# Windowed attention, gated convolution and gated values on one core: scores in four 64x64 tiles, batch 0 turned by transposes, a tap and the split of v on GpSimd

## The chip, the cores and the metric

The kernel runs on one core of one Trainium2 chip. The metric is device time in microseconds (us). A core has TensorE (PE: matrix products into the accumulators, PSUM, which has 8 banks), VectorE (DVE), ScalarE (ACT), GpSimd (POOL, which does not read PSUM) and SyncE (SP, which here issues all DMAs). PEld is PE's loading of its stationary operand.

## The reference

Three layers, for 4 batches of 576 positions, in float32:

```python
# 1: attention, 8 heads of 64, window 128, linear bias by distance
scores = scale * np.matmul(q, k.transpose(0, 1, 3, 2))
mask = (rel >= 0) & (rel < window)
scores = np.where(mask, scores + bias[None], -1000000000.0)
attn = np.exp(scores - np.max(scores, axis=-1, keepdims=True))
attn = attn / (np.sum(attn, axis=-1, keepdims=True) + 1e-09)
x = np.matmul(attn, v)                       # heads side by side: 512 columns
# 2: h = relu(x @ w_in), 1024 wide; 3 taps along the positions; gate; back to 512
h = np.maximum(x @ w_in, 0.0)
x = h * sigmoid(conv(h, 3 taps)) @ w_out
# 3: value x @ w_val, gated by 5 causal taps over x; out
out = sigmoid(causal_conv(x, 5 taps)) * (x @ w_val) @ w_out2
```

## The kernel before

Features lie on the 128 partitions, positions along the columns. The work is cut into 8 units: 4 batches, each in a first half (positions 0 to 255, `u` = 0) and a second (the rest, `u` = 1). For a unit the loop at L849 records `hidden` (product `win`, ReLU, three taps, gate), `mixed` (product `wout`, five taps), `valued` (product `wval`, times the gate) and `output` (product `wo`, and the DMA of the result), and the attention of the unit after it. Float32 operands of these dense products are split into a high and a low part (fp32r), and L691 to L693 are the three products high x high, high x low, low x high; the weights are split (`widen`, L376) while batch 0 runs. A weight tile comes by DMA into one of three `raw` buffers, ACT writes a part of it into a PSUM bank of `ring_pw`, DVE shifts the other part (L390) and joins the two (L401), and ACT and POOL split the result.

`attention` takes a pair of heads (`p`) and a half. Positions go in blocks of 64, four in the first half and five in the second; a block sees at most 192 keys, and the first two of a sequence 64 and 128. For a block, both heads are computed at once: the stationary matrix (L538) is 128x128 with the queries of one head in one quarter, those of the other in the opposite one, and zeros elsewhere. Two blocks share one of three score banks (`pss`). Then DVE adds the bias and takes the maximum (L542), ACT takes the exponential and its sum (L550), POOL and DVE make the reciprocal (L555, L560). In batches 1 to 3 the rows are scaled and split into two float16 parts (L598, L600), and DMA transposes turn them (L609). In batch 0 (`turn`) they stay in float32 and PE turns them: a product with a diagonal matrix `dg` scales and turns 128 columns at once (L568, L569, L576), and ACT copies the result to `pt`. The value product (L640) uses 128x64 tiles, one head in each half of the array's columns. Its v is float32 in batch 0; after that it is scaled and split into two float16 parts, in most pairs by ACT (L515) and DVE (L355), in eight by ACT and POOL (L509, L512).

The dense products take PSUM banks `pm` in turn: four, but two for the first 16 products, as the other two (`ring_pw`) then serve the weights.

The order is not the order of the code. Each step is recorded with its engine (or several to choose from), an estimated duration, its reads and writes, and a priority. `forward` simulates the engines and takes the readiest step of the best priority; `backward` sets priorities from the end of a simulated run; `order` repeats this 7 times and keeps the best run. The engines then run that fixed order. Where the simulated PE would be idle before 80 us, `warm` puts fillers there: products of an idle tile (L868).

Of the kernel before, what the change touches and what calls it, by code (L numbers as in the profile page):

```python
# [40 lines left out]
class Program:  # L41
# [28 lines left out]
    def forward(self):  # L70
# [24 lines left out]
        while n < len(self.ops):  # L95
# [19 lines left out]
            if o.bank is not None and o.bank in held:  # L115
                x, until = held[o.bank]
                if x != e and until > t:
                    heapq.heappush(wait[e], (until, o.seq, o))
                    continue
            if e == "SP" and dma - t > BACKLOG:  # L120
                heapq.heappush(wait[e], (dma - BACKLOG, o.seq, o))
                continue
            o.eng, o.dur, o.fn = next(a for a in o.alts if a[0] == e)
            out.append(o)
            if e == "PE":
                if tiled and not o.drain:
                    t += 85.0
# [68 lines left out]
    def order(self):  # L196
# [21 lines left out]
BACKLOG = 2500.0  # L218
SLOW = {"DVE": 0.72, "POOL": 0.15}
# [27 lines left out]
def attention_moe_moe_kernel(  # L247
# [51 lines left out]
    ring_raw = Ring("raw", RAWS, [128, 2 * WC], U32)  # L299
    ring_g = Ring("g", 11, [128, 2, GMAX], F32R)  # L300
# [75 lines left out]
    def widen(src, cols, hi, lo, hk, lk, prio):  # L376
# [8 lines left out]
        tk = ps_m.name + str(2 + ring_pw.at)  # L385
# [90 lines left out]
    def attention(b, u, p, prio, step):  # L476
# [27 lines left out]
        if not turn:  # L504
# [21 lines left out]
        groups = [[0, 1], [2, 3]] if nb == 4 else [[0, 1], [2, 3], [4]]  # L526
        for gi, g in enumerate(groups):
            gp, sk = ps_s.next()
            a, e = g[0], g[-1] + 1
            pr = prio + step * (e - 1)  # L530
            blk = []
            for i in g:
                j = j0 + i
                nkey = 64 * min(j + 1, 3)
                blk.append((i, gp[:, 192 * (i - a):192 * (i - a) + nkey], nkey, 64 * (max(0, j - 2) - k0)))

            def scores(blk=blk):
                return [nc.tensor.matmul(out=o, lhsT=q_t[:, i, :], rhs=k_t[:, kc:kc + nkey], start=True, stop=True,  # L538
                                         skip_group_check=True) for i, o, nkey, kc in blk]
            pg.add("PE", sum(mm4_t(b_[2]) for b_ in blk), scores, pr, (qk,), ((sk, 0), (sk, 1)))  # L540
            for i, s, nkey, _ in blk:
                pg.add("DVE", 128 + 1.05 * nkey, lambda i=i, s=s, nkey=nkey: nc.vector.tensor_tensor_reduce(  # L542
                    out=s, in0=s, in1=bm[:, p, 192 - nkey:192], op0=ALU.add, op1=ALU.min,
                    scale=-0.125, scalar=3.0e38, accum_out=stt[:, 0, i:i + 1]), pr, ("bm",), ((sk, i - a), (stk, 0, i)), bank=sk)
            for i, s, nkey, _ in blk:
                to, tok = s, ()
                if turn:
# [4 lines left out]
                    accum_out=stt[:, 1, i:i + 1]), pr, ((stk, 0, i), "pz" + pk[1:]), ((sk, i - a), (stk, 1, i)) + tok, bank=sk)  # L552
# [388 lines left out]
```

## Time and profile before

| | |
|---|---|
| median of 3 runs | 439.55 us (438.98 to 440.91) |
| the profiled execution | 438.07 us, its span 436.3 us |
| busy: PE, DVE, ACT, POOL | 421.0, 323.4, 302.6, 194.7 us |
| granted clock of TensorE | 1.0 in all 40 slices |
| chain that ended last | PE 77%, DVE 10%, POOL 4%, ACT 3%, DMA 3% |

A busy time counts a moment once, however many instructions overlap in it. Matmuls are pipelined: a duration of one is from its start to the end of its drain, and what one costs in a stream is the distance between starts. The page's share of the chain is time on the path that ended last; the stages show where each engine is near full.

### The profile page before, as it was taken

How to read it: one execution, taken by the hardware profiler on the slowest of the kernel's cores; microseconds unless marked ns; L12 is line 12 of the kernel's file. 1: busy time of each engine (PE TensorE's matmuls, PEld its weight loads, DVE VectorE, ACT ScalarE, POOL GpSimd, SP SyncE). 2: the span in 40 equal slices, each digit the busy share in tenths (PEclk: the TensorE clock that was granted, in tenths of full speed). 3: DMA queues.
4: the chain of work that ended last, by engine and by line, in shares of the span. 5: the costliest groups of instructions: out<-in, count | busy, mean ns of one | idle time of the engine just before them, and what ended most of it. 6: DMA issues, size and time to landing. Idle time of an engine off the chain costs nothing.

```text
span 436.3 us, 9827 instructions
## 1 busy us (share of the span) xinstructions
PE 421.0 (96%) x3433; PEld 401.5 (92%) x3433; DVE 323.4 (74%) x1000; ACT 302.6 (69%) x894; POOL 194.7 (45%) x341
## 2 busy tenths in 40 slices
PE   7879899899999999999999999999999999999996
PEld 7669788799999999999999999999999999999996
DVE  4799998987857488947888288938888498817480
ACT  5779787755858586857968587648856687848442
POOL 2568899732634063213713274234604073536311
PEclk9999999999999999999999999999999999999999
DMA  8878566769016437471446337482544446540001
GB/s 278 271 248 287 189 205 224 223 191 233 14 62 109 123 96 169 88 192 36 97 114 134 114 75 175 90 189 86 77 94 107 132 112 137 86 109 0 2 0 63
DMA packets 74738, 57.05 MB, mean 131 GB/s; under 512 B 56000, under 2 KB 65472, under 8 KB 74688
## 3 DMA queue, kind: packets, MB, share of 16 engines
q1 hardware_dynamic: 74688, 56.42, 49.7%
q8 instruction: 27, 0.44, 0.4%
q14 instruction: 23, 0.19, 0.1%
HBM read 38.32 MB, written 4.72 MB: 99 GB/s over the span
## 4 chain that ended last, share of the span: by engine, by line
PE 77%; DVE 10%; POOL 4%; ACT 3%; DMA 3%; issue 2%; SPq 0%; DVEq 0%; ACTq 0%
PE pm L691 22%; PE pm L692 20%; PE pm L693 20%; PE pss L538 8%; PE psx L640 5%; DVE t L355 2%; DVE pss L542 1%; DVE raw L390 1%; DVE dg L568 1%; DVE gts L401 1%; DMA raw<-in_vN 1%; POOL g L370 1%; DMA pt<-p 1%; DVE vmx L435 1%; PE pss L576 1%
## 5 line engine op out<-in xcount | busy, mean ns | idle before, releaser
L691 PE MATMUL pm<-x,win 128*128 128x256 f32 (+1 forms) x256 | 80.0, 313 | 0.4 <-DVE t L355 0.3
L691 PE MATMUL pm<-g,wout 128*128 128x254 f32 (+1 forms) x256 | 80.0, 313 | 0.1
L692 PE MATMUL pm<-g,wout 128*128 128x254 f32 (+1 forms) x256 | 76.2, 297 | 0.0
L692 PE MATMUL pm<-x,win 128*128 128x256 f32 (+1 forms) x256 | 76.1, 297 | 0.0
L693 PE MATMUL pm<-x,win 128*128 128x256 f32 (+1 forms) x256 | 75.8, 296 | 0.0
L693 PE MATMUL pm<-g,wout 128*128 128x254 f32 (+1 forms) x256 | 75.7, 296 | 0.0
L355 DVE SCALAR_TENSOR_TENSOR t<-pm,cc,t 128x325 f32<-128x325 f32 (+3 forms) x112 | 56.7, 515 | 16.3 <-ACT t L348 12.9
L370 POOL TENSOR_TENSOR g<-t,g 128x254 fp32r<-128x254 f32 (+1 forms) x64 | 52.2, 818 | 33.0 <-ACT g L339 30.1
L538 PE MATMUL pss<-qk 128*128 128x192 f32 (+2 forms) x288 | 57.8, 326 | 3.2 <-ACT pt L348 2.1
L355 DVE SCALAR_TENSOR_TENSOR gts<-pm,cc,gts 128x322 f32<-128x322 f32 (+4 forms) x120 | 58.7, 512 | 0.6
L542 DVE CUSTOM_DVE_ANT_0 pss<-pss,bm 128x192 f32<-128x192 f32 (+2 forms) x144 | 48.4, 342 | 10.3 <-PE pss L538 7.8
L550 ACT ACTIVATE pss<-pss,st 128x192 f32<-128x192 f32 (+2 forms) x108 | 41.0, 380 | 14.2 <-DVE st L542 12.5
L691 PEld LDWEIGHTS pm<-x,win 128*128 128x128 f32 x256 | 48.2, 188 | 2.7 <-DVE t L355 1.2
L538 PEld LDWEIGHTS pss<-qk 128*128 128x128 f32 x288 | 45.5, 195 | 5.3 <-ACT pt L348 3.2
L691 PEld LDWEIGHTS pm<-g,wout 128*128 128x128 f32 x256 | 48.2, 188 | 2.2 <-DVE gts L355 1.1
L693 PEld LDWEIGHTS pm<-g,wout 128*128 128x128 f32 x256 | 48.6, 190 | 0.0
L692 PEld LDWEIGHTS pm<-g,wout 128*128 128x128 f32 x256 | 48.6, 190 | 0.0
L692 PEld LDWEIGHTS pm<-x,win 128*128 128x128 f32 x256 | 48.2, 188 | 0.0
L693 PEld LDWEIGHTS pm<-x,win 128*128 128x128 f32 x256 | 48.2, 188 | 0.0
L600 DVE SCALAR_TENSOR_TENSOR p<-pss,st,p 128x192 f16<-128x192 f32 (+1 forms) x103 | 36.4, 388 | 15.1 <-DMA pt<-p 8.9
L555 POOL TENSOR_SCALAR st<-st 128x2 f32<-128x2 f32 (+1 forms) x80 | 16.0, 200 | 69.0 <-ACT pss L550 58.7
L370 POOL TENSOR_TENSOR g<-gts,g 128x254 fp32r<-128x254 f32 (+1 forms) x32 | 26.0, 817 | 37.1 <-ACT g L339 36.3
(100 smaller groups left out, 1092.7 us busy)
## 6 DMA issues: line engine op xcount, KB each, us to landing
qk<-in_qk SPq DMA_DIRECT2D x16, 544.0 KB, 4.0
qk<-in_qk SPq DMA_DIRECT2D x16, 384.0 KB, 3.5
raw<-in_w_out SPq DMA_DIRECT2D x12, 512.0 KB, 4.3
raw<-in_w_in SPq DMA_DIRECT2D x8, 512.0 KB, 5.1
vr<-in_vN SPq DMA_DIRECT2D x14, 256.0 KB, 3.0
out<-t SPq DMA_DIRECT2D x16, 161.0 KB, 1.8
raw<-in_vN SPq DMA_DIRECT2D x6, 384.0 KB, 3.8
raw<-in_w_val SPq DMA_DIRECT2D x4, 512.0 KB, 4.4
```

The lines of the kernel that those rows point to most:

```text
L355: pg.add("DVE", dve_t(n, 0 if isinstance(scalar, float) else 1), lambda: nc.vector.scalar_tensor_tensor(out=out, in0=in0, scalar=scalar, i ...
L370: "POOL": (pool_t(n, True), lambda: nc.gpsimd.tensor_tensor(out=lo, in0=src, in1=hi.bitcast(F32), op=ALU.subtract))}
L390: pg.add("DVE", dve_t(cols, fast=True), lambda: nc.vector.tensor_scalar(low, low, 29, None, op0=ALU.logical_shift_right), prio, (rk,), (rk ...
L538: return [nc.tensor.matmul(out=o, lhsT=q_t[:, i, :], rhs=k_t[:, kc:kc + nkey], start=True, stop=True, skip_group_check=True) for i, o, nke ...
L542: pg.add("DVE", 128 + 1.05 * nkey, lambda i=i, s=s, nkey=nkey: nc.vector.tensor_tensor_reduce(out=s, in0=s, in1=bm[:, p, 192 - nkey:192], ...
L550: pg.add("ACT", act_t(nkey, True, 2), lambda i=i, s=s, to=to: nc.scalar.activation(out=to, in_=s, func=AF.Exp, scale=-1.0, bias=stt[:, 0, ...
L555: "POOL": (165, lambda a=a, e=e: nc.gpsimd.tensor_scalar(stt[:, 2, a:e], stt[:, 1, a:e], 1e-9, norm, op0=ALU.add, op1=ALU.mult))}
L600: pg.add("DVE", dve_t(nkey, 1), lambda i=i, s=s, hi=hi, lo=lo: nc.vector.scalar_tensor_tensor(out=lo, in0=s, scalar=stt[:, 2, i:i + 1], in ...
L640: r.append(nc.tensor.matmul(out=oap, lhsT=lhs, rhs=rhs, start=(i == first[h]), stop=(i == last[h]), skip_group_check=True))
L691: return [nc.tensor.matmul(out=o, lhsT=wh, rhs=hi, start=first, stop=False), nc.tensor.matmul(out=o, lhsT=wh, rhs=lo, start=False, stop=Fa ...
L692: nc.tensor.matmul(out=o, lhsT=wh, rhs=lo, start=False, stop=False),
L693: nc.tensor.matmul(out=o, lhsT=wl, rhs=hi, start=False, stop=last)]
```

## The change

- `attention`: in batches 1 to 3 the first four blocks of a half are one group (`quad`). Each block is two 64x64 products (one head each, no zeros), both written to the block's bank; blocks 0 and 2 use one score bank, 1 and 3 another, so a group holds two of the three. In odd blocks the heads' places in the partitions are exchanged, with a second bias table `bx` (loaded into `raw2` once the weights are in) and other offsets in the value product. The fifth block of the second half is done as before.
- batch 0: the exp rows are scaled in place on DVE, POOL or ACT, and turned by PE transposes with the unit matrix; the `dg` ring goes, and `p` has two buffers.
- `mixed`: the first tap added (k = 3) goes by ACT and POOL in every batch, not in batch 0 alone. v's scaling, cast and subtraction are all POOL's in batches 1 to 3.
- the dense products have three banks for the first 16, and the weights one.
- the planner: DVE steps on the port shared with POOL do not start under a POOL step and the two exclude each other; other estimates for the scores and the turns; 41 simulated runs, from the tenth on with random changes to the priorities.

```diff
@@ forward
+            if e == "DVE" and o.port and using["POOL"] > t + SPIN:
+                heapq.heappush(wait[e], (using["POOL"] - SPIN, o.seq, o))
+                continue
...
-                if tiled and not o.drain:
+                if tiled and tiled != o.drain:
                     t += 85.0
...
-                x = "DVE" if e == "POOL" else "POOL"
-                both = max(0.0, using[x] - t)
...
+                t = max(t, using["DVE" if e == "POOL" else "POOL"])
@@ order
-        for i in range(1 + 6):
+        rng = random.Random(1)
+        for i in range(1 + 40):
             if i:
                 self.backward(span)
+            if i > 8:
+                for o in self.ops:
+                    o.prio += rng.gauss(0.0, 200.0)
@@ buffers
+    ring_vm = Ring("raw", 0, None, None)
+    ring_vm.t = ring_raw.t[0:2]
+    bx = ring_raw.t[2][:, 0:NP * 96].bitcast(BF16).rearrange("q (p n) -> q p n", n=192)
...
-    ring_p = Ring("p", 1, [128, 2, 10, 128], F16)
-    ring_dg = Ring("dg", 3, [128, 128], F32)
+    ring_p = Ring("p", 2, [128, 2, 10, 128], F16)
...
-    ps_m.spare = (16, 16)
+    ps_m.spare = (16,)
...
-    ring_pw.t = ps_m.t[2:4]
+    ring_pw.t = ps_m.t[3:4]
@@ attention: v
-            if nth_a in (18, 20, 21, 23, 24, 29, 30, 31):
-                pg.add("ACT", act_t(n, False, 1), lambda: nc.scalar.activation(out=vin, in_=vin, func=AF.Copy, scale=s_up),
+            if nth_a > 7:
+                pg.add("POOL", pool_t(n,False,1), lambda: nc.gpsimd.tensor_scalar(vin, vin, s_up, 0.0, op0=ALU.mult, op1=ALU.add),
                        prio, ((sck, 1),), vkeys)
-                cast(vin, v1, n, prio, vkeys, ((vk, 1), vk))
+                cast(vin, v1, n, prio, vkeys, ((vk, 1), vk), ('POOL',))
@@ attention: scores
+            held = [ps_s.next() for _ in range(2 if four else 1)]
...
+                o, ok = held[i % 2] if four else held[0]
+                c = 192 * (i // 2 if four else i - a)
...
+                    for h in range(2):
+                        x = h ^ (i % 2)
+                        r.append(nc.tensor.matmul(
+                            out=o[64 * x:64 * x + 64], lhsT=q_t[64 * h:64 * h + 64, i, 64 * h:64 * h + 64],
+                            rhs=k_t[64 * h:64 * h + 64, kc:kc + nkey], start=True, stop=True, skip_group_check=True))
@@ attention: batch 0
-                        lambda dg=dg, ri=ri: nc.vector.tensor_scalar(dg, eye, ri, None, op0=ALU.mult),
-                        lambda dg=dg, ri=ri: nc.gpsimd.tensor_scalar(dg, eye, ri, 0.0, op0=ALU.mult, op1=ALU.add)),
+                        lambda row=row, ri=ri: nc.vector.tensor_scalar(row, row, ri, None, op0=ALU.mult),
+                        lambda row=row, ri=ri: nc.gpsimd.tensor_scalar(row, row, ri, 0.0, op0=ALU.mult, op1=ALU.add),
+                        lambda row=row, ri=ri: nc.scalar.activation(out=row, in_=row, func=AF.Copy, scale=ri)),
...
-                        return [nc.tensor.matmul(out=gp[:, 128 * (x - 2 * a):128 * (x - 2 * a) + 128], lhsT=pe_[:, 128 * x:128 * x + 128],
-                                                 rhs=dg, start=True, stop=True, skip_group_check=True) for x in sl]
+                        return [nc.tensor.transpose(gp[:, 128 * (x - 2 * a):128 * (x - 2 * a) + 128], pe_[:, 128 * x:128 * x + 128], eye)
+                                for x in sl]
@@ mixed
-                    k in ((3,) if b == 0 else ()), yk)
+                    k == 3, yk)
```

On PE, at scores of a first half among dense products; before this is batch 2 (`pss` is a score bank, `qk` a pair's queries and keys, `x` and `g` inputs of dense products; x2 is a count):

```order
L693 MATMUL pm_119<-x_88,win_62 128x328
L538 MATMUL pss_124<-qk_103 128x64
L538 MATMUL pss_124<-qk_103 128x128
L691 MATMUL pm_120<-x_92,win_61 128x328
L692 MATMUL pm_120<-x_92,win_61 128x328
L693 MATMUL pm_120<-x_92,win_62 128x328
L691 MATMUL pm_120<-x_88,win_61 128x328
L692 MATMUL pm_120<-x_88,win_61 128x328
L693 MATMUL pm_120<-x_88,win_62 128x328
L538 MATMUL pss_125<-qk_103 128x192 x2
L538 MATMUL pss_123<-qk_104 128x64
```

On PE after the change, at scores of batch 1:

```order
L726 MATMUL pm_119<-g_82,wout_63 128x254
L727 MATMUL pm_119<-g_82,wout_64 128x254
L562 MATMUL pss_123<-qk_103 64x64 x2
L562 MATMUL pss_121<-qk_103 64x128 x2
L562 MATMUL pss_123<-qk_103 64x192 x2
L562 MATMUL pss_121<-qk_103 64x192 x2
L725 MATMUL pm_119<-g_83,wout_63 128x254
L726 MATMUL pm_119<-g_83,wout_63 128x254
L727 MATMUL pm_119<-g_83,wout_64 128x254
```

A pair's four blocks stood apart, two in one bank and two in the next, with dense products between; now the eight products of four blocks stand together, in two banks.

On DVE in batch 0, at the first weights and the softmax of the first pairs; before (`st` holds maxima, sums and reciprocals, `raw` weights, `cc` and `gts` joined weights):

```order
L568 TENSOR_SCALAR dg_115<-eye,st_111 128x128
L542 ISA pss_125,st_112<-pss_125,bm 128x128
L542 ISA st_112 128x1
L401 SCALAR_TENSOR_TENSOR cc<-pm_121,raw_74 128x44
L390 TENSOR_SCALAR raw_75<-raw_75 128x512
L560 RECIPROCAL st_111<-st_111 128x2
L401 SCALAR_TENSOR_TENSOR gts<-pm_122,raw_75 128x512
```

On DVE after the change, at the same place:

```order
L597 TENSOR_SCALAR p_113<-p_113,st_111 128x64
L396 TENSOR_SCALAR raw_75<-raw_75 128x512
L396 TENSOR_SCALAR raw_74<-raw_74 128x44
L588 RECIPROCAL st_111<-st_111 128x2
L597 TENSOR_SCALAR p_113<-p_113,st_111 128x192
L407 SCALAR_TENSOR_TENSOR cc<-pm_120,raw_74 128x44
```

The diagonal matrix is gone from DVE's order; it scales a row of `p` here instead, and the weights' shifts come in pairs ahead of their joins. Of the 36 rows, 8 stand on DVE, 11 on POOL and 17 on ACT; PE's order has 122 fillers where it had 85.

On POOL, in the second half of batch 0, as v of batch 1 is prepared; before (`vr` is v as loaded, `v` its two parts, `vsc` its scale):

```order
L370 TENSOR_TENSOR g_86<-t_98,g_86 128x326
L678 CAST x_90<-x_91 128x2x8
L370 TENSOR_TENSOR g_87<-t_99,g_87 128x326
L366 TENSOR_TENSOR t_101<-t_101,t_93 128x326
L370 TENSOR_TENSOR g_77<-t_100,g_77 128x326
L555 TENSOR_SCALAR st_111<-st_111 128x2
```

On POOL after the change, at the same place:

```order
L515 TENSOR_SCALAR vr_105<-vr_105,vsc 128x256
L347 TENSOR_SCALAR v_106<-vr_105 128x256
L376 TENSOR_TENSOR g_87<-t_99,g_87 128x326
L518 TENSOR_TENSOR v_106<-vr_105,v_106 128x256
L712 CAST x_90<-x_91 128x2x8
L372 TENSOR_TENSOR t_101<-t_101,t_93 128x326
L376 TENSOR_TENSOR g_77<-t_100,g_77 128x326
```

The three steps of v stand between the splits of the gated products and ahead of `x`'s copy; the normalisation that ends the first piece comes later in the order.

## Rows read from the trace of the kernel before

**Rows 1.** The page: busy us, share and instructions by engine; the chain by engine.
```profile
PE 421.0 (96%) x3433; PEld 401.5 (92%) x3433; DVE 323.4 (74%) x1000; ACT 302.6 (69%) x894; POOL 194.7 (45%) x341
...
PE 77%; DVE 10%; POOL 4%; ACT 3%; DMA 3%; issue 2%; SPq 0%; DVEq 0%; ACTq 0%
```
**Rows 2.** Stages (us from:to): length, busy and instructions by engine, granted clock, DMA.
```profile
0.00:24.00 24.00, 18.67 (x130) 15.78 (x131) 15.17 (x58) 15.25 (x50) 11.07 (x29) 1.00 0.82 278
24.00:62.60 38.60, 34.77 (x290) 30.63 (x288) 36.40 (x106) 32.47 (x94) 31.24 (x45) 1.00 0.73 235
62.60:83.20 20.60, 18.65 (x161) 17.41 (x159) 17.46 (x49) 16.36 (x40) 18.20 (x27) 1.00 0.66 218
83.20:145.00 61.80, 61.55 (x455) 58.92 (x455) 47.50 (x136) 40.35 (x119) 25.26 (x41) 1.00 0.52 126
145.00:376.00 231.00, 230.90 (x1975) 223.92 (x1975) 177.95 (x589) 167.38 (x518) 86.57 (x167) 1.00 0.49 113
376.00:436.30 60.30, 56.42 (x430) 54.83 (x428) 28.88 (x68) 30.81 (x77) 22.40 (x35) 1.00 0.23 47
```
**Rows 3.** The chain in order of time, batch 0 to 1: start, us, what.
```profile
127.43 0.65 PE pss L538 x4
...
128.98 0.44 PE pss L538 x4
```
**Rows 4.** Timeline of PE around a value product in batch 0: start, us, what.
```profile
83.98 0.28 PE L693 MATMUL pm<-g,wval 128*128 128x254 f32 x1
84.19 1.32 PE L640 MATMUL psx<-pt,v 128*64 128x128 f32 x20
...
85.67 0.28 PE L692 MATMUL pm<-g,wval 128*128 128x254 f32 x1
```
**Rows 5.** The turns, as a group (busy, mean ns), and eight in the timeline.
```profile
L576 PE MATMUL pss<-dg,p 128*128 128x128 f32 x128 | 19.1, 283 | 1.8 <-POOL dg L569 1.1 <-DVE dg L568 0.8
...
35.24 1.05 PE L576 MATMUL pss<-dg,p 128*128 128x128 f32 x8
36.13 0.58 PE L868 MATMUL psx<-idle 128*128 128x192 bf16 x5
```
**Rows 6.** Twelve fillers in the timeline, and what follows them.
```profile
15.65 1.15 PE L868 MATMUL psx<-idle 128*128 128x192 bf16 x12 [0.93 <-ACT x L655]
16.64 1.81 PE L576 MATMUL pss<-dg,p 128*128 128x128 f32 x12
```
**Rows 7.** Lines: ns min/median/max, first and last; then groups: busy, mean ns.
```profile
L568 DVE TENSOR_SCALAR dg<-eye,st x18: 273/600/1336, 7.5 to 75.7; 128x128 f32<-128x128 f32 x18
L390 DVE TENSOR_SCALAR raw<-raw x25: 190/424/1528, 6.3 to 80.5; 128x512 uint32<-128x512 uint32 x24, 128x44 uint32<-128x44 uint32 x1
...
L568 DVE TENSOR_SCALAR dg<-eye,st 128x128 f32<-128x128 f32 x18 | 10.8, 621 | 0.7 <-PE pss L576 0.7
L390 DVE TENSOR_SCALAR raw<-raw 128x512 uint32<-128x512 uint32 x24 | 15.9, 664 | 0.0
L339 ACT ACTIVATE p<-t 128x192 f16<-128x192 f32 x3 | 1.0, 364 | 0.0
```
**Rows 8.** Timeline of POOL and DVE at 41.7 us.
```profile
41.66 1.27 POOL L370 TENSOR_TENSOR wout<-gts,wout 128x512 fp32r<-128x512 f32 x1
41.70 1.53 DVE L390 TENSOR_SCALAR raw<-raw 128x512 uint32<-128x512 uint32 x1
```
**Rows 9.** Groups of the widening on ACT and DVE.
```profile
L401 DVE SCALAR_TENSOR_TENSOR gts<-pm,raw 128x512 uint32<-128x512 uint32 x24 | 16.2, 680 | 1.8 <-POOL wval L370 1.2 <-ACT pm L392 0.3
...
L392 ACT ACTIVATE pm<-raw 128x512 f32<-128x512 f32 (+1 forms) x25 | 15.5, 625 | 0.1
```
**Rows 10.** Groups on POOL: a tap's addition, the cast and subtraction of v.
```profile
L366 POOL TENSOR_TENSOR gts<-gts,t 128x253 f32<-128x253 f32 (+1 forms) x8 | 6.8, 846 | 7.3 <-ACT t L365 7.3
...
L341 POOL TENSOR_SCALAR v<-vr 128x512 f16<-128x512 f32 x5 | 3.1, 620 | 6.0 <-ACT t L348 3.0 <-ACT vr L509 2.5 <-PE psx L640 0.4
L512 POOL TENSOR_TENSOR v<-vr,v 128x512 f16<-128x512 f32 x6 | 7.0, 1166 | 0.3
```

More of the change, by code (lines that the diff above doesn't have):

```diff
@@ L1 @@
+import random
 from contextlib import ExitStack
@@ L218 @@
 BACKLOG = 2500.0
+SPIN = 150.0
+XP = 75.0
 SLOW = {"DVE": 0.72, "POOL": 0.15}
@@ L384, in widen @@
         pw, _ = ring_pw.next()
[L385 removed]
+        tk = ps_m.name + str(3 + ring_pw.at)
         r = raw.rearrange("p (n w) -> p n w", w=2)
@@ L428, in vmax @@
         for pp in groups:
-            raw, rk = ring_raw.next()
+            raw, rk = ring_vm.next()
             np_ = len(pp)
@@ L525, in attention @@
         norm = 1.0 if turn else 1.0 / PSC
-        groups = [[0, 1], [2, 3]] if nb == 4 else [[0, 1], [2, 3], [4]]
+        quad = not turn
+        if quad:
+            groups = [[0, 1, 2, 3]] if nb == 4 else [[0, 1, 2, 3], [4]]
+        else:
+            groups = [[0, 1], [2, 3]] if nb == 4 else [[0, 1], [2, 3], [4]]
         for gi, g in enumerate(groups):
-            gp, sk = ps_s.next()
             a, e = g[0], g[-1] + 1
             pr = prio + step * (e - 1)
-            blk = []
+            four = len(g) == 4
+            held = [ps_s.next() for _ in range(2 if four else 1)]
+            gp, sk = held[0]
+            blk, on = [], {}
+            every = tuple((y, x) for _, y in held for x in range(2))
             for i in g:
@@ L534, in attention @@
                 nkey = 64 * min(j + 1, 3)
[L535 to L540, printed above, removed]
+                o, ok = held[i % 2] if four else held[0]
@@ new lines, in attention, with scores @@
+                c = 192 * (i // 2 if four else i - a)
+                on[i] = (ok, i // 2 if four else i - a)
+                blk.append((i, o[:, c:c + nkey], nkey, 64 * (max(0, j - 2) - k0)))
+            def scores(blk=blk, four=four):
+                r = []
+                for i, o, nkey, kc in blk:
+                    if not four:
+                        r.append(nc.tensor.matmul(out=o, lhsT=q_t[:, i, :], rhs=k_t[:, kc:kc + nkey], start=True, stop=True,
+                                                  skip_group_check=True))
+                        continue
+                    for h in range(2):
[3 more added lines that the diff above has]
+                            rhs=k_t[64 * h:64 * h + 64, kc:kc + nkey], start=True, stop=True, skip_group_check=True))
+                return r
@@ L541, in attention @@
+            dur = sum(max(mm4_t(x[2]) for x in blk[y:y + 2]) for y in (0, 2)) + 60 if four else sum(mm4_t(b_[2]) for b_ in blk)
+            pg.add("PE", dur, scores, pr, (qk,), every).drain = "quad" if four else False
             for i, s, nkey, _ in blk:
-                pg.add("DVE", 128 + 1.05 * nkey, lambda i=i, s=s, nkey=nkey: nc.vector.tensor_tensor_reduce(
-                    out=s, in0=s, in1=bm[:, p, 192 - nkey:192], op0=ALU.add, op1=ALU.min,
-                    scale=-0.125, scalar=3.0e38, accum_out=stt[:, 0, i:i + 1]), pr, ("bm",), ((sk, i - a), (stk, 0, i)), bank=sk)
+                tab, tk = (bx, (("bx", 0), ("bx", 1))) if four and i % 2 else (bm, ("bm",))
+                pg.add("DVE", 75 + 1.05 * nkey, lambda i=i, s=s, nkey=nkey, tab=tab: nc.vector.tensor_tensor_reduce(
+                    out=s, in0=s, in1=tab[:, p, 192 - nkey:192], op0=ALU.add, op1=ALU.min,
+                    scale=-0.125, scalar=3.0e38, accum_out=stt[:, 0, i:i + 1]), pr, tk, (on[i], (stk, 0, i)), bank=on[i][0])
@@ L581, in attention @@
                 to = pt32[:, s0:slots[-1] + 1:st_, :]
-                scaled(to, src, 1.0, 128 * sn, pr, ((sk, 0), (sk, 1)), ((ptk, 0, gi),), ("ACT",), True, sk)
+                scaled(to, src, 1.0, 128 * sn, pr, every, ((ptk, 0, gi),), ("ACT",), True, sk)
                 continue
@@ L847, in attention_moe_moe_kernel @@
         load(n)
+    for x in range(2):
+        sync(lambda x=x: nc.sync.dma_start(out=bx[64 * x:64 * x + 64], in_=bias[64 - 64 * x:128 - 64 * x]),
+             90000.0, (), (("bx", x), "raw2", "raw2l"), 273.0)
     t, todo = T0, UNITS
```

30 lines of the change are left out of this document (15 added, 15 removed).

## The prediction, made before the changed kernel had run

> **What bounds the kernel now.** I read the busy times of the engines first, then those by stage, then the chain of waits, and only then single pieces. TensorE (PE) is busy 96% of the span, and the chain that ended last is 77% PE [rows 1]. The stages say where this holds. I cut the span where batch 0, first half of the positions, begins its val product (83.2 us) and at 376 us, where the last attention work ends. Between the two, PE is busy 292.45 of 292.8 us while VectorE (DVE) has 225 and GpSimd (POOL) 112: what PE is spared there comes off the end, and what another engine is spared is worth nothing [rows 2]. Before 83.2 us it is otherwise: in 24 to 62.6 us DVE is busy 36.4 of 38.6 us (94%), against 90, 84 and 81% for PE, ACT and POOL; and part of PE's work in these early stages is fillers on an idle tile [rows 2, 6]. So the change is two sums: PE work after 83.2 us, and the length of the stage before it.
>
> **Scores in 64x64 tiles.** Batches 1 to 3 have 12 head pairs for each half. Today two score blocks of 192 keys cost PE 0.65 us and a pair of 64 and 128 keys 0.44 [rows 3]; four blocks are 0.65 + 0.65 = 1.30 us in the second half of the positions and 0.44 + 0.65 = 1.09 in the first. Each block multiplies a 128x128 matrix that is half zeros. The change does eight 64x64 products instead, and they are meant to run four at a time: two rounds, 2 x 0.325 = 0.65 us in the second half, and in the first half a round of at most 128 keys (0.22) and one of 192 (0.325), 0.54.
>
> The trace has no 64x64 tiles, but it has 128x64 ones, in the value product of batch 0. From 83.98 to 85.67 us stand one dense step before, twenty instructions, and one dense step after; with 0.12 us for each of the two steps, the visit takes 1.45 us [rows 4]. Each head has 640 columns, which at 0.325/192 = 1.69 ns a column is 1.08 us. Two heads one after the other would be 2.17. So the two halves of the array do work at once, and a visit to another tile shape costs about 1.45 - 1.08 = 0.37 us for leaving the dense stream and coming back. With that a four-block group costs 0.65 + 0.37 = 1.02 (saves 0.28) or 0.54 + 0.37 = 0.91 (saves 0.18), and 12 x 0.46 = 5.5 us come off. The fifth block of the second half stays as it is.
>
> Bounds. If the visits cost nothing, 12 x (0.65 + 0.55) = 14.4 us come off. If only two products run at a time, groups cost 1.30 + 0.37 and 1.09 + 0.37, and 12 x 0.74 = 8.9 us are added. If none overlap, 2.60 + 0.37 and 2.18 + 0.37: 12 x 3.1 = 38 us added. I take 5.5, since the nearest row shows halves of the array overlapping.
>
> Here a rule of the Trainium skill speaks against the change. TensorEngine Tiling (Array Packing), section Gotcha 1: PSUM Pressure, says that tiles on different rows of the array write different PSUM banks and cannot reach one bank at the same time. The diff puts both heads of a block, which are different row tiles, into one bank (in different partitions); by the rule as worded they would take turns, and the sum would be the +8.9 us above instead of -5.5. The rows here show column tiles alone, so they neither bear it out nor refute it.
>
> **Turning by transposes, batch 0.** There are 64 of these 128x128 turns, each two instructions [rows 5]. Eight instructions take 36.13 - 35.24 = 0.89 us, or 0.22 a turn [rows 5]. The trace has no transpose on PE; I take one instruction for the two, 0.11, the middle between no gain (two instructions as now) and 14.2 us (free): 64 x 0.11 = 7.1 us less PE work. All of it lies before 83.2 us. The order also has 122 fillers where there were 85; a filler costs (16.64 - 15.65)/12 = 0.083 us [rows 6], so 3.1 us come back. PE's stream before 83.2 us is 4.0 us shorter, if nothing else holds it.
>
> The diagonal matrices go: 18 on DVE, 10.8 us, and 18 on POOL. DVE's cost a mean of 621 ns and at best 273 [rows 7]; the excess is waiting for POOL, as in the shift of 1.53 us that ends 0.30 us after the POOL operation it started beside [rows 8]. In their place the 36 exp rows are scaled: 8 on DVE, 11 on POOL, 17 on ACT by the order. At 0.36 us on ACT and 0.42 on DVE (the nearest rows, a cast of 192 columns and the median shift [rows 7]) DVE gets back 3.4 us and ACT 6.2. The 24 shifts of the weights have a median of 424 ns and a mean of 664 [rows 7]; the new planner no longer starts DVE work on that port under a POOL operation, and of 24 x 0.24 = 5.8 us I take half. DVE's sum before 83.2 us, 69.0 us [rows 2], falls by 10.8 - 3.4 + 2.9 = 10.3. ACT's, 64.1, rises by 6.2, less some 2 for four scalings by channel weights that the order moves off it.
>
> What is late next: ACT. In 24 to 62.6 us it would have about 35 busy us (32.5, 3.6 for ten of the rows, less 1), and filled as densely as DVE is now (94%) needs 37.3 of the 38.6. So the stage shrinks by at least 1.3 us and at most by what DVE loses, 10.3; the middle is 5.8, and PE's own 4.0 lies beside it. I take 6. Two edits are inside this number. The dense products of the first half of batch 0 (16 of them) get three banks instead of two, so a product can begin while two others still are read. The widening of the weights gets one bank instead of two: a bank is held for an ACT pass of 0.63 us and a DVE pass of 0.68 [rows 9], so 24 in a row need at least 24 x 1.31 = 31 us of the 83, and they wait more tightly on DVE. Two buffers for the exp rows let one pair's exponentials start before the other's are turned.
>
> **One tap, and v's split, to POOL.** In batches 1 to 3, 24 taps leave DVE; each becomes an ACT pass and a POOL addition of 0.85 us [rows 10]. All 24 splits of v go to POOL: a scaling and a cast at 0.62 us and a subtraction of 1.17 for 512 columns, 2.4 us [rows 10], and some 1.5 for 256. Together 24 x 0.85 + 12 x 2.4 + 12 x 1.5 = 67 us, less some 12 for the eight splits that POOL has now. POOL after 83.2 us rises from 134 to 189 of 353 us, 54% [rows 2]. I price it at nothing: PE's dense stream covers it. Behind a split on POOL's queue wait the normalisation of softmax, and with it the copies and DMA transposes, and then PE. The cover is gone when the order's lead is less than the 2.4 us; 24 such waits of half that would cost 29 us, and the low end is nothing.
>
> **The sum.** The profiled execution took 438.07 us (span 436.3): 438.07 - 5.5 - 6.0 = 426.6. The median of the runs, 439.55, is 1.5 above the profiled one, so I predict 428.0 us, and 423 to 433 for this case by itself.
>
> **Rivals.**
> *Batch 0 keeps its length.* ACT takes DVE's place, or the single bank makes the widening late, and only the scores pay: 439.5 - 5.5 = 434. For it speaks that ACT and POOL are above 80% in the middle stage; against it, that nothing there is added to POOL and PE loses work.
> *Batch 0 gives all that DVE loses.* 10.3 us, and the visits to the score tiles share their cost with those of the value product beside them, a third of 24 x 0.37 (3 us): 439.5 - 10.3 - 5.5 - 3 = 420.7. For it speak the 94% of DVE and the stalls on POOL.
> *Tiles take turns.* In the four-block groups of batches 1 to 3 only two products run at once; +8.9 there and -6 in batch 0 give 442.5, slower. It decides from where the 24 groups cost more than 28.7 us (now) + 6 = 34.7, or 1.45 us for one. Speaking against it are the overlapping halves [rows 4].
> *PE waits in the stream.* A group takes two of the three score banks until all four blocks are read, where a pair took one, and normalisation queues behind v's split. If each of the 24 groups makes PE wait 0.4 us, 9.6 us go: 428 + 9.6 = 437.6. Against it: PE's stream idles 0.35 us of 292.8 now.
>
> **Chances.** Forecast 0.55; batch 0 unchanged 0.19; all of DVE 0.14; tiles in turn 0.08; PE waits 0.04. A difference within 0.5% (2.2 us) can't be told from none. The forecast, the second and the third case are faster but for about 0.04 at the edge: 0.84. That edge and the last case are the same: 0.08. Tiles in turn are slower: 0.08. The range takes in the first three cases and the last: 419 to 438.
>
> **What would show it.** In the changed profile: score groups of 0.9 to 1.1 us in the chain, with four instructions starting almost together; from the first val product on, PE still without idle; that product at about 77 us instead of 83.2; transposes of one instruction at about 0.11 us; DVE below 90% and ACT near 90% in the middle stage; POOL near 245 us busy. The forecast is wrong if groups take over 1.45 us, if idle time of PE after 83 us passes 3 us, or if the first val product is no earlier.

## The result, and the profile after

The changed kernel takes 433.09 us (median of four runs, 430.77 to 434.29) against 439.55: a ratio of 0.984, 95% interval 0.981 to 0.987. It is faster, by 6.5 us where 11.5 were forecast; 433.1 lies in the range of 419 to 438, and just outside the forecast's own 423 to 433. The profiled execution took 433.56 us (span 431.8).

The page's busy times and TensorE clock (40 slices), and the chain by engine; they answer to [rows 1]:

```profile
PE 413.1 (96%) x3598; PEld 382.5 (89%) x3598; DVE 305.6 (71%) x941; ACT 296.1 (69%) x900; POOL 239.8 (56%) x392
...
PEclk9999989999999999999999999999999999999999
...
PE 67%; DVE 15%; DMA 6%; ACT 5%; issue 3%; POOL 2%; ACTq 0%; DVEq 0%; POOLq 0%
```

PE is as full as before, but its share of the chain is down from 77% to 67%, and one slice of the clock is below full. The stages cut as in [rows 2] (length, then PE, PEld, DVE, ACT, POOL, the granted clock, DMA):

```profile
24.00:62.60 38.60, 33.78 (x282) 30.46 (x282) 32.82 (x96) 33.53 (x98) 28.33 (x42) 0.96 0.71 232
62.60:83.20 20.60, 19.59 (x188) 17.61 (x187) 17.69 (x52) 17.24 (x46) 16.74 (x22) 1.00 0.66 215
83.20:145.00 61.80, 58.08 (x445) 53.74 (x444) 46.51 (x127) 38.47 (x115) 32.25 (x52) 1.00 0.53 137
145.00:376.00 231.00, 229.63 (x2189) 213.90 (x2188) 169.75 (x560) 165.21 (x529) 127.34 (x216) 1.00 0.51 116
```

Before, PE idled 0.35 us between 83.2 and 376 us; now it idles 61.80 - 58.08 + 231.00 - 229.63 = 5.1. In the middle stage DVE is down from 94% to 85%, ACT is at 87%, and the clock is 0.96.

The pieces that the prediction had priced, from PE's timeline and (the last row) from the chain, where a piece counts only its time on the path:

```profile
77.25 0.28 PE L725 MATMUL pm<-g,wval 128*128 128x254 f32 x1
...
237.37 0.31 PE L727 MATMUL pm<-g,wo 128*128 128x322 f32 x1
237.61 0.88 PE L562 MATMUL pss<-qk 64*64 64x192 f32 x16
238.42 0.42 PE L725 MATMUL pm<-g,wo 128*128 128x322 f32 x1
238.67 0.32 PE L726 MATMUL pm<-g,wo 128*128 128x322 f32 x1
```
```profile
59.52 0.66 PE pss L606 x6
```

The first val product stands at 77.25 us, where about 77 was forecast. From 237.37 to 238.67 us lie two dense steps of 0.15 us and a score group: 1.30 - 0.30 = 1.00 us for four blocks (forecast 1.02; two pairs took 1.30). The first instructions of its four tiles start 6 to 7 ns apart. The same reading of the first half's groups gives 0.90 (forecast 0.91). A transpose takes 0.66 / 6 = 0.11 us (taken as 0.11).

So both terms of the sum arrived, and some was given back. I number PE's dense steps in order of time, the first as 0; a batch has 576. Step 576, where batch 0 is over by count, begins at 147.5 us (148.2 before): of the 6.0 us won at the val product, 5.3 are lost again by then. From there to the start of the last dense step it takes 280.6 us instead of 284.3. Two places in batch 0 stand out. The first, in windows:

```profile
48.00:51.00 3.00, 3.00 (x34) 2.77 (x29) 3.00 (x10) 2.98 (x11) 3.00 (x4) 1.00 0.84 240
51.00:54.40 3.40, 0.03 (x2) 0.03 (x1) 3.33 (x10) 3.37 (x11) 3.07 (x6) 1.00 0.89 282
54.40:58.10 3.70, 3.70 (x25) 3.43 (x25) 2.46 (x6) 2.79 (x8) 3.54 (x4) 0.54 0.80 230
58.10:61.00 2.90, 2.90 (x27) 2.90 (x27) 1.72 (x4) 0.79 (x2) 0.67 (x2) 1.00 0.55 167
```
```profile
54.37 3.70 PE L905 MATMUL psx<-idle 128*128 128x192 bf16 x23 [3.37 <-DVE x L691]
```

PE stands still for 3.4 us: the next things on its queue are 23 fillers, and these wait for DVE to read the value product out of the bank that they write. Then they run at a granted clock of 0.54, that is nearly at the lower level, 1.2 GHz, and take 3.70 us (0.16 each against 0.083 in [rows 6]), with the `wout` products behind them. The second place is 93 to 131 us; before, then after:

```profile
93.00:131.00 38.00, 37.84 (x274) 36.65 (x273) 28.94 (x72) 24.61 (x66) 14.56 (x20) 1.00 0.41 105
93.00:131.00 38.00, 34.73 (x269) 31.17 (x268) 31.59 (x85) 25.23 (x75) 18.64 (x30) 1.00 0.60 152
```

The stretch from step 288 to step 480 takes 38.3 us where it took 32.4. Its waits, in brackets:

```profile
95.99 0.42 PE L725 MATMUL pm<-x,win 128*128 128x328 f32 x1 [0.62 <-ACT t L354]
100.64 0.38 PE L456 MATMUL psx<-eye,vmx 128*4 128x128 f32 x2 [0.97 <-DVE vmx L450]
...
107.33 0.38 PE L470 MATMUL psx<-vdg,one 4*128 4x8 f32 x2 [0.45 <-DVE vdg L466]
122.95 0.30 PE L674 MATMUL psx<-pt,v 128*64 128x256 f16 x2 [1.05 <-DMA pt<-p]
```

Two of them, 1.42 of these 3.09 us, are the scale of v, which needs the maxima loaded through two raw buffers, one fewer than before.

### The profile page after: what moved, and what is told of

It is laid out like the page before. It is cut to its first block, busy times and chain, and to the rows that moved or that the text cites. A ratio compares the mean times of both kernels' runs of the same rounds, so it can differ in the third digit from the quotient of the medians.

```text
span 431.8 us, 10151 instructions
## 1 busy us (share of the span) xinstructions
PE 413.1 (96%) x3598; PEld 382.5 (89%) x3598; DVE 305.6 (71%) x941; ACT 296.1 (69%) x900; POOL 239.8 (56%) x392
## 4 chain that ended last, share of the span: by engine, by line
PE 67%; DVE 15%; DMA 6%; ACT 5%; issue 3%; POOL 2%; ACTq 0%; DVEq 0%; POOLq 0%
PE pm L725 19%; PE pm L726 17%; PE pm L727 17%; PE psx L674 4%; DMA raw<-in_vN 4%; DVE t L361 4%; PE pss L562 4%; PE pss L557 3%; DVE gts L361 2%; PE psx L905 2%; DVE pss L570 2%; DMA pt<-p 1%; DVE gts L407 1%; ACT p L578 1%; ACT pm L761 1%
## 5 line engine op out<-in xcount | busy, mean ns | idle before, releaser
L361 DVE SCALAR_TENSOR_TENSOR gts<-pm,cc,gts 128x322 f32<-128x322 f32 (+3 forms) x96 | 47.0, 508 | 2.0 <-POOL gts L372 0.8
L372 POOL TENSOR_TENSOR gts<-gts,t 128x253 f32<-128x253 f32 (+1 forms) x32 | 25.8, 806 | 28.4 <-ACT t L371 18.0
L630 DVE SCALAR_TENSOR_TENSOR p<-pss,st,p 128x192 f16<-128x192 f32 (+2 forms) x103 | 35.9, 386 | 7.8 <-ACT p L628 7.5
L570 DVE CUSTOM_DVE_ANT_0 pss<-pss,bm 128x192 f32<-128x192 f32 (+2 forms) x96 | 32.4, 342 | 11.4 <-PE pss L557 8.2
L725 PE MATMUL pm<-g,wval 128*128 128x254 f32 (+1 forms) x128 | 39.6, 310 | 0.2 <-ACT g L345 0.2
L725 PE MATMUL pm<-g,wo 128*128 128x254 f32 (+1 forms) x128 | 38.9, 304 | 0.3 <-DVE gts L820 0.3
L726 PE MATMUL pm<-g,wo 128*128 128x254 f32 (+1 forms) x128 | 38.1, 298 | 0.2 <-POOL g L376 0.2
```

Source lines behind the costliest of these rows:

```text
L361: pg.add("DVE", dve_t(n, 0 if isinstance(scalar, float) else 1), lambda: nc.vector.scalar_tensor_tensor(out=out, in0=in0, scalar=scalar, i ...
L372: pg.add("POOL", pool_t(n, True), lambda: nc.gpsimd.tensor_tensor(out=out, in0=out, in1=t, op=ALU.add), prio, (tk,), (key,))
L570: pg.add("DVE", 75 + 1.05 * nkey, lambda i=i, s=s, nkey=nkey, tab=tab: nc.vector.tensor_tensor_reduce(out=s, in0=s, in1=tab[:, p, 192 - nk ...
L630: pg.add("DVE", dve_t(nkey, 1), lambda i=i, s=s, hi=hi, lo=lo: nc.vector.scalar_tensor_tensor(out=lo, in0=s, scalar=stt[:, 2, i:i + 1], in ...
L725: return [nc.tensor.matmul(out=o, lhsT=wh, rhs=hi, start=first, stop=False), nc.tensor.matmul(out=o, lhsT=wh, rhs=lo, start=False, stop=Fa ...
L726: nc.tensor.matmul(out=o, lhsT=wh, rhs=lo, start=False, stop=False),
```

## The experiments

The theory at the start: quads are worth 5.5 us, and what was lost sits in the late maxima of v. Rivals: quads bring little; POOL's split of v holds PE up; the order drawn by the planner decides. All times are medians beside runs of the kernel before (439.2 to 439.6 us).

**E1, full scores.**

```diff
-        quad = not turn
+        quad = False
```

> The changed kernel, with the scores of batches 1 to 3 in 128x128 products of two blocks as before; everything else as changed. Theory (quads are worth what the sum says, 24 groups x 0.23 = 5.5 us, and what was lost sits elsewhere): 433.1 + 5.5 = 438.6 us, a group of four blocks 1.30 and 1.09 us in two pieces. Rival (the visits to the small tiles break the stream, so the quads bring nothing net): 433 us or less.

434.62 us, ratio 0.988 (0.985 to 0.990): 1.5 us slower than the changed kernel, not 5.5. Neither side is settled, since the planner drew another order. In it the stretch from step 288 to 480 takes 34.3 us, with two buffers for the maxima.

**E2, three buffers for the maxima.**

```diff
-    ring_vm.t = ring_raw.t[0:2]
-    bx = ring_raw.t[2][:, 0:NP * 96].bitcast(BF16)...
+    ring_vm = ring_raw
+    bx = st("bx", [128, NP, 192], BF16)
```

Other tiles are trimmed to make room, and the planner draws another order.

> The changed kernel with the second copy of the bias in a tile of its own, so that the loads for the maxima of v have three raw buffers as before instead of two (room for it is made by trimming spare columns of other tiles). Theory (the 5 us that the front won and batch 0's second half gave back come from the late maxima of v): the stretch from the 288th to the 480th dense step, 38.2 us in the changed kernel and 32.4 before, returns to 33 to 35 us, PE's idle time there falls from 3.3 to under 1.5 us, and the whole takes 428 to 430 us. Rival 1 (v's split and the tap on POOL hold PE up): 433 us, the stretch stays at 38. Rival 2 (chance of the order found by the planner): the stretch may move either way, the total by 2 us or so.

432.87 us, ratio 0.984 (0.980 to 0.989). The stretch is 33.5 us instead of 38.3, and PE's idle time there is nearly gone:

```profile
93.00:131.00 38.00, 37.80 (x292) 34.90 (x291) 28.77 (x71) 26.02 (x72) 19.46 (x31) 1.00 0.52 131
```

The total didn't follow. The profiled run, the fastest of the four, reaches step 576 at 143.9 us, 3.6 earlier than the changed kernel's, but its 430.69 us at mean clock 1.0 are no less than the changed kernel's 430.77 in its own run at 1.0. For the stretch the theory of the maxima isn't shown either: E1, E3, E4 and E8 keep two buffers, and in their orders it takes 34.3 to 35.0 us; E11's, also with two, takes 37.9, and none of its waits there of over 0.3 us is for the maxima.

This order has PE gaps of 2.5 and 2.1 us. In this run the clock is at its upper level behind both; the first, and what follows it:

```profile
15.70:18.20 2.50, 0.00 (x0) 0.00 (x0) 2.33 (x10) 2.50 (x9) 1.32 (x5) 1.00 0.95 286
18.20:22.00 3.80, 3.79 (x39) 3.78 (x39) 1.50 (x5) 2.32 (x7) 1.75 (x4) 1.00 0.84 327
```

**E3, another draw.**

```diff
-        rng = random.Random(1)
+        rng = random.Random(2)
```

> The changed kernel with another seed for the planner's random disturbance of priorities, nothing else. Theory (late maxima of v): total 431 to 435 us, the stretch from the 288th to the 480th dense step stays at 37 us or more. Rival (the loss is an accident of the order drawn): the stretch falls below 35 us and the total moves by more than 3 us.

428.20 us (428.0 to 428.4), ratio 0.974 (0.971 to 0.976). The same edits in another order take what was forecast. The stretch is 34.7 us with two buffers. The middle stage:

```profile
24.00:62.60 38.60, 36.83 (x317) 33.33 (x317) 35.29 (x105) 36.58 (x105) 31.88 (x45) 1.00 0.75 252
```

PE is 95% busy where it was 88%, the clock stays at 1.00, and ACT, which the prediction named as late next, is at 95%.

**E4, v as before.**

```diff
-            if nth_a > 7:
-                pg.add("POOL", ... vin, vin, s_up ...)
+            if nth_a in (18, 20, 21, 23, 24, 29, 30, 31):
+                pg.add("ACT", ... vin, vin, s_up ...)
```

> The changed kernel with v's split as before (ACT casts and DVE subtracts for 16 head pairs, ACT scales and POOL subtracts for 8), everything else as changed. Theory (v's split on POOL is covered, the loss is the late maxima): 432 to 434 us, and the stretch from the 288th to the 480th dense step stays at about 38 us. Rival (POOL's split of 2.4 us sits on the path in batch 1, PE waits of 0.7 us at 159 and 0.4 us at 304 and the idle time at 122 are its work): 429 to 431 us, and these waits are gone.

432.13 us, ratio 0.982 (0.976 to 0.988), from 428.7 to 434.6: undecided. The stretch from step 288 to 480 is 35.0 us, not the 38 of the theory, though the maxima still have two buffers. It too has a PE gap (2.1 us at 70 us).

**E5, full scores in E3's order.** Every instruction keeps its place; a group issues four 128x128 products (bias table and value offsets to match).

```diff
-                    for h in range(2):
-                        x = h ^ (i % 2)
-                        r.append(nc.tensor.matmul(out=o[64 * x:64 * x + 64], ...64x64...))
+                    r.append(nc.tensor.matmul(out=o, lhsT=q_t[:, i, :], rhs=k_t[:, kc:kc + nkey], ...))
```

> The kernel of the other draw (428.2 us), instruction for instruction in the same order, with the four blocks of a score group multiplied as four 128x128 products instead of eight 64x64 ones. Theory (a group costs PE 0.90 and 1.01 us against 1.09 and 1.30, so quads are worth 12 x 0.19 + 12 x 0.29 = 5.8 us once the order is held): 433.5 to 434.5 us. Rival (the first experiment's 1.5 us is all that quads are worth, since DVE or the softmax chain sets the pace anyway): 429.5 to 430 us.

431.98 us, ratio 0.982 (0.978 to 0.986): quads are worth 3.8 us, between the theory and the rival. PE's busy time, full scores first, then E3:

```profile
PE 417.2 (97%) x3399; PEld 397.6 (92%) x3399; DVE 306.1 (71%) x938; ACT 299.1 (70%) x904; POOL 238.9 (56%) x391
```
```profile
PE 410.5 (96%) x3591; PEld 380.6 (89%) x3591; DVE 304.9 (71%) x938; ACT 298.8 (70%) x904; POOL 239.0 (56%) x391
```

A group costs 1.09 and 1.30 us here, 0.90 and 1.00 there: 12 x 0.19 + 12 x 0.30 = 5.9 us. The missing 2 us are a new wait: PE idles 3.6 us behind batch 0 with quads and 1.5 without, and of the waits after 140.4 us in E3's profile the largest for PE is (us, times, longest)

```profile
PE psx L674 <- DMA pt<-p: 2.5, 3, 1.0
```

a wait that the list of E5 doesn't have: PE now reaches some value products before the DMA transposes of the weights of attention have landed.

**E6, without the late fillers,** in the changed kernel's order.

```diff
+        if t > 30000.0 and end - t > 2500.0:
+            return
         while t + 250.0 < end:
```

> The changed kernel in the same order without the 23 fillers that it issues at 54.4 us (fillers in a planned gap of over 2.5 us after 30 us are left out). Theory (these fillers wait for the copy of a value product out of their bank, start 3.4 us late, run at the lower clock and hold up the first layer's product behind them): the 96th dense step is unmoved, the 192nd comes 2 to 4 us earlier than at 77.2 us, and the total falls by 2 to 3 us, to 430 to 431. Rival (VectorE sets the pace of this stage, so PE waits as long without them, and the clock falls for longer): 433 to 435 us.

430.80 us, ratio 0.979 (0.973 to 0.985), from 428.5 (mean clock 1.0) to 432.8 (0.991). In the profiled run the dense products themselves pay:

```profile
51.60:55.50 3.90, 0.10 (x2) 0.04 (x1) 3.83 (x10) 3.65 (x13) 3.69 (x5) 0.88 0.87 273
55.50:59.00 3.50, 3.50 (x16) 3.50 (x17) 2.43 (x7) 3.20 (x8) 3.21 (x5) 0.50 0.76 240
59.00:63.00 4.00, 4.00 (x26) 4.00 (x25) 3.02 (x5) 1.85 (x5) 3.03 (x5) 0.70 0.47 180
```
```profile
55.47 0.58 PE L725 MATMUL pm<-g,wout 128*128 128x254 f32 x1 [3.81 <-DVE t L361]
```

Without fillers the gap is as long (3.8 us), with VectorE busy in 3.83 of the 3.90, and the lower clock lasts longer. The first val product stands at 77.6 us in this run (77.25 with the fillers), against the theory: PE's next dense product waits for VectorE, as the rival said. The median is 2.3 us below the changed kernel's, as the theory said, but the intervals overlap.

**E7, the planner's part alone** (port rule, 41 plans) in the kernel before.

```diff
+            if e == "DVE" and o.port and using["POOL"] > t + SPIN: ...
-        for i in range(1 + 6):
+        for i in range(1 + 40):
+            if i > 8:  o.prio += rng.gauss(0.0, 200.0)
```

> The kernel before with the planner's part of the change alone: no DVE work started on the shared port under a POOL operation, the search over 41 plans instead of 7 with disturbed priorities. Theory (the search and the port rule shorten the early stage, quads and transposes make up the rest): 436 to 439 us. Rival (the order's chance is all that moved the front): 433 us or less. A third possibility, that the rule alone is worth nothing: 439 to 440.

436.13 us, ratio 0.992 (0.988 to 0.995): some 3 us come with the planner's part alone, in the one order that it drew. Its first val product is early and the stretch behind it is not:

```profile
79.48 0.37 PE L694 MATMUL pm<-g,wval 128*128 128x254 f32 x1
```
```profile
93.00:131.00 38.00, 35.44 (x253) 33.03 (x252) 31.07 (x85) 23.32 (x68) 14.01 (x21) 1.00 0.54 126
```

The val product comes 3.8 us earlier than before, and step 576 at 148.5 us: all of it is given back, with three buffers for the maxima, no quads and v's split as before. The stretch from step 288 to 480 takes 36.2 us (this profile is of the slowest of the seven runs, 438.40 us). The weights' shifts, a mean of 664 ns in [rows 7], take

```profile
L393 DVE TENSOR_SCALAR raw<-raw 128x512 uint32<-128x512 uint32 x24 | 12.9, 537 | 1.1 <-DMA raw<-in_w_in 0.8 <-DMA raw<-in_w_val 0.2
```

or 24 x 0.127 = 3.0 us less of DVE (2.9 taken).

**E8, a third draw** (`random.Random(3)`).

> The changed kernel with a third seed for the planner's disturbance. Theory (the order drawn moves the total by several us, and 433 of the changed kernel is one draw from about 428 to 434): between 427 and 435 us; where PE has no idle time over 2 us in batch 0 the clock stays at its upper level and the time is in the lower half of that. Rival (428.2 was the exception): 432 to 434 us.

428.45 us, ratio 0.975 (0.970 to 0.979): E3 was no exception. PE idles no less here than in the changed kernel:

```profile
83.20:145.00 61.80, 60.60 (x473) 56.13 (x475) 42.17 (x118) 37.37 (x110) 30.54 (x49) 1.00 0.57 145
145.00:376.00 231.00, 226.86 (x2162) 211.35 (x2159) 168.57 (x562) 168.11 (x540) 124.76 (x212) 1.00 0.51 114
```

That is 1.20 + 4.14 = 5.3 us. But step 192 begins at 74.1 us (77.25 in the changed kernel), and the stretch from step 288 to 480 takes 34.8 us.

**E9, a gap put into the third draw.** E6's edit in E8's order takes away 24 fillers:

```profile
51.18 2.14 PE L905 MATMUL psx<-idle 128*128 128x192 bf16 x24 [0.53 <-DVE x L691]
```

> The third draw (428.45 us, clock 0.998 to 1.0, no idle time of PE over 1.2 us) in the same order, without the 24 fillers that it issues at 51.2 us; nothing else. Theory (what costs the changed kernel and the first, fourth and sixth experiments 2 to 4 us in most of their runs is the lower clock after a PE idle time of over 2 us): PE idles about 2.5 us at 51 us, most runs show a mean clock of 0.991 to 0.996, the dense steps behind the gap run at half speed for 3 us or more, and the median rises to 430 to 432 us with a wider spread. Rival (the clock is not tied to the gap, it varies by itself): 428 to 429 us and 0.998 to 1.0 as in the third draw.

430.19 us, ratio 0.979 (0.975 to 0.982), 1.7 more than E8, and mean clocks of 0.988 to 0.996 in all four runs (E8: 0.998 to 1.0). In this order the lower clock comes with the gap; the price is less sure, as the intervals overlap, and of the two profiled runs E9's is the shorter (428.96 against 429.89 us). Its windows:

```profile
46.00:50.30 4.30, 4.30 (x44) 3.66 (x42) 4.27 (x14) 4.30 (x17) 4.30 (x8) 1.00 0.64 215
50.30:53.00 2.70, 0.08 (x2) 0.10 (x1) 2.70 (x8) 2.42 (x6) 2.54 (x4) 1.00 0.78 288
53.00:56.00 3.00, 3.00 (x17) 3.00 (x18) 3.00 (x7) 2.68 (x7) 2.84 (x5) 0.58 0.76 247
56.00:60.00 4.00, 4.00 (x30) 4.00 (x30) 1.98 (x9) 2.46 (x5) 3.33 (x5) 0.89 0.60 209
```

The same stretch in E8:

```profile
53.00:56.00 3.00, 3.00 (x27) 2.84 (x26) 3.00 (x8) 2.94 (x8) 2.84 (x5) 1.00 0.64 216
```

27 instructions on PE at the full clock, 17 at 0.58. Here fillers were what kept the clock up. In the changed kernel 23 come too late and run for 3.7 us, though without them (E6) the val product comes no earlier. Over all kernels (longest PE idle time in batch 0's first half from 8 us on; mean clocks of the runs):

```text
changed 3.4 us: 0.995 0.995 0.996 1.0      E3  1.0 us: 0.999 0.999 1.0 1.0
E1      2.3 us: 0.996 0.996 0.996 1.0      E5  1.0 us: 1.0 in all four
E2      2.5 us: 0.992 0.996 0.996 1.0      E8  0.9 us: 0.998 0.998 1.0 1.0
E4      2.1 us: 0.991 0.996 0.996 0.999    E10 1.1 us: 0.999 1.0 1.0 1.0
E6      3.8 us: 0.991 0.992 0.995 1.0      E12 0.9 us: 0.999 0.999 1.0 1.0 1.0 1.0
E9      2.6 us: 0.988 0.994 0.994 0.996    E7  1.3 us: 0.996 0.999 0.999, 1.0 in four
E11     2.3 us: 0.996 0.996 0.998 1.0
```

**E10, v cast twice,** in E8's order.

```diff
-  lambda: nc.gpsimd.tensor_scalar(hi, src, 1.0, 0.0, ...)
+  lambda: [nc.gpsimd.tensor_scalar(hi, src, 1.0, 0.0, ...) for _ in range(2 if mode == ('POOL',) else 1)]
```

> The third draw (428.45 us) in the same order, with POOL's cast of v issued twice in a row in each of the 24 head pairs of batches 1 to 3: POOL has some 12 us more to do, and each split is 0.4 to 0.6 us longer. Theory (PE's dense stream covers the split of v on POOL): 428 to 429 us. Rival (the split is on the path: scaling, cast and subtraction hold up the normalisation behind them and then PE): half or more of the 12 us show, 434 us or more.

431.94 us, ratio 0.984 (0.980 to 0.989): 3.5 of POOL's 12.6 extra us (236.3 to 248.9 busy) show. Neither nothing nor half. Whether they show through POOL's queue or through the port that the planner treats as shared with DVE isn't told apart.

**E11, a fourth draw** (`random.Random(9)`).

> The changed kernel with a fourth seed (the ninth number). Theory (without a PE idle time over 2 us in batch 0 the change is worth what its parts add up to, whichever order is drawn): 426.5 to 430 us if PE has no such gap; 430 to 434 with most runs below a mean clock of 0.997 if it has one. Rival (the draws differ by several us for other reasons): outside these ranges.

431.71 us, ratio 0.982 (0.978 to 0.987). It has a gap, and the time is in the theory's range for that, but two of the four runs, not most, are below 0.997, and in the profiled run (0.996) the clock doesn't fall at the gap:

```profile
30.36 0.82 PE L905 MATMUL psx<-idle 128*128 128x192 bf16 x8 [2.28 <-DVE x L691]
...
106.14 0.42 PE L725 MATMUL pm<-x,win 128*128 128x328 f32 x1 [1.39 <-DVE t L361]
```
```profile
28.10:30.40 2.30, 0.04 (x1) 0.03 (x1) 1.83 (x7) 2.30 (x11) 1.77 (x5) 1.00 0.97 331
30.40:34.00 3.60, 3.60 (x35) 2.92 (x35) 1.71 (x5) 2.59 (x8) 1.32 (x3) 1.00 0.37 117
104.80:107.60 2.80, 1.46 (x9) 1.25 (x9) 2.80 (x16) 2.58 (x10) 2.01 (x3) 1.00 0.09 36
107.60:111.00 3.40, 3.40 (x14) 3.40 (x14) 2.43 (x7) 2.39 (x8) 2.66 (x6) 0.50 0.13 9
```

Behind the gap of 2.28 us it stays at 1.00; the lower level comes 77 us later, 1.5 us after a wait of 1.39 us. The one run at 1.0 took 429.24.

**E12, v cast on ACT,** in E8's order: the same place in the program, `nc.scalar.activation` instead of `nc.gpsimd.tensor_scalar`.

> The third draw (428.45 us) with every instruction at the same place of the program, but the 24 casts of v in batches 1 to 3 issued on ACT instead of POOL: the mirror of the tenth experiment, in which some 12 us more on POOL cost 3.5 us. Theory (v's split on POOL sits on the path for a part of its length, so POOL's time there costs about 0.3 us for each us): 425 to 427.5 us, the fastest of all. Rival 1 (only the longer split of the tenth experiment crossed the order's lead; at its own length it is covered): 428 to 429 us. Rival 2 (ACT, which then waits for POOL's scaling in the middle of its queue, holds up the exponentials): over 430 us.

428.48 us, ratio 0.973 (0.970 to 0.975), with POOL at 224.6 us busy: the same as E8, and my expectation of a gain missed. That fits a split that is covered at its own length, but ACT's 9.1 us more (299.8 to 308.9 busy) could also have taken back a gain. E10 shows that 0.5 us more a split is not covered.

## Why the prediction was right or wrong

*Scores in 64x64 tiles:* right in mechanism and price. 0.90 and 1.00 us a group against 0.91 and 1.02; the overhead of a visit, read from the value product as 0.37 us, is 0.35 to 0.36 at another tile shape. At the end of the kernel 3.8 of 5.9 us arrive (E5, in E3's order), since PE then waits for transposes; the prediction had argued that what PE is spared there "comes off the end" and didn't ask what comes late next in that stage.

*Tiles take turns:* refuted by the 1.00 us (1.45 was its point). The rule of the Trainium skill that spoke for it (TensorEngine Tiling (Array Packing), Gotcha 1: PSUM Pressure) says that different row tiles cannot access the same bank at the same time. As worded it doesn't hold here; the measurement decides. By the diff the two row tiles of a block write one bank on different partitions, and as odd blocks have their heads swapped, the two that write the same partitions have different banks. The Trainium skill's PSUM — Partial Sum Buffer, section PSUM bank collisions raise a hardware error, quotes the wide rule too, and beside it has as measured that two row tiles writing one bank and one 32-partition quadrant raise an error. The trace agrees with the narrower one as far as it goes: row tiles on different partitions of one bank run together. Two row tiles in the same bank and partitions weren't tried.

*Batch 0:* -6.0 at the first val product, as forecast, and by the steps named: transposes 0.11, shifts -2.6 us of DVE (24 x (0.664 - 0.557); 2.9 taken), DVE 85%, ACT 87% (near 90 forecast). In E7 the planner's part alone brings 3.8 of the 6.0, which the prediction counted only by the shifts. That is one order each, so the share is an estimate.

*The step that failed* is "from the first val product on, PE still without idle". Rows show 5.1 us of idle time there, past the 3 that the prediction had set as its mark. It had named the rival "PE waits in the stream" (437.6, chance 0.04), but by score banks and the normalisation behind v's split. What came stands in the second half of batch 0: the stretch from step 288 to 480 takes 5.9 us more than before, 3.1 of them in four waits, on ACT, on the DMA transposes and, for 1.4 us, on the maxima of v. The maxima's two buffers aren't shown to be the cause, since four other orders with two take 34.3 to 35.0 us, a fifth 37.9 without waiting for them (E11), and E7 with three takes 36.2.

Idle time alone doesn't make the 433 either: E8 has 5.3 us of it and takes 428.45, with a front 3.2 us earlier and a shorter stretch. What the prediction lacked is a term for the order drawn: the same edits take 428.2, 428.45, 431.7 and 433.1 us in four orders (E3, E8, E11 and the changed kernel).

A part of the 5.1 us between forecast and result is the clock, and the price taken for the fillers with it: 122 at 0.083 us each, of which 23 cost 0.16. In the profiled run 3.70 us at 0.54 are 3.70 x 0.46 = 1.7 us of full-clock work lost; they lie before the val product, which came as forecast all the same. The one run of the changed kernel at mean clock 1.0 is 2.3 us below the median, but that is one run, and the kernel before takes from 438.1 to 441.8 us in runs at 1.0. E9 gives 1.7 for a gap, with overlapping intervals. The rest goes with the order drawn. How much of it is the stretch, and how much the front's later step 288 (93.3 us against 89.1 and 88.6 in E3 and E8), stays open: E2 shortened the first and the front moved too.

That E3 and E8 hit 428 is partly luck of signs. There step 576 begins at 140.4 and 140.0 us, 8 us earlier than before and not 6, and what follows takes 282.5 and 284.1 us, where 5.5 less than 284.3 were forecast.

*Tap and v on POOL:* priced at nothing, and E12 fits that for v's cast, without excluding a gain that ACT took back; the cover is thin (E10). The tap alone wasn't tried.

## What to carry to other kernels

Where a planner draws an order, a change is measured together with its draw: try two or three seeds before a few us are put down to an edit, and hold the order fixed (same places, other instructions) to price one. Work that keeps TensorE's clock up must not wait for anything: a filler that writes a bank someone still reads stands still exactly when it is needed, and then runs in front of the real work (23 fillers for 3.7 us here). A saving on the busiest engine is worth its price only up to the next thing that arrives late.

## What the hardware showed

- Four 64x64 tiles run side by side with two banks between them: eight products of 192 columns in 1.00 us, the visit included (E5's four full ones: 1.30).
- The lower clock goes with PE gaps, but a gap doesn't decide it. In the seven kernels whose profile has a gap of 2.1 to 3.8 us in batch 0's first half, 21 of 28 runs have a mean clock below 0.997; in the other six beside the kernel before, 1 run of 29. In five of the seven profiles the clock falls within the gap or up to 1.2 us behind it. In E2's it stays up behind two gaps, and in E11's it stays up behind 2.28 us and falls after 1.39. The same instructions give 0.995 in one run and 1.0 in another.
- In five of the six kernels that have both a run below 0.997 and one at 0.999 or 1.0 among these seven, the run with the highest clock is the fastest (E6: 428.5 us at 1.0, 432.8 at 0.991); in E1 it is the slowest. The kernel before, longest gap 1.5 us, has 6 of 35 runs below 0.997; they take 1.3 us more on average (440.8 against 439.5).
